# Six load buffers instead of four, and the first six pairs asked for at once, in cosine attention followed by a two-layer leaky-ReLU product

## The chip, the cores and the metric

The kernel runs on one core of a Trainium2 chip. The metric is the device time of one execution in microseconds. TensorE multiplies matrices and writes to PSUM (eight banks); VectorE (DVE), ScalarE (ACT) and GpSimd (POOL) do the elementwise work; SyncE (SP) only issues transfers. Sixteen DMA engines carry all transfers; they are asked for from SP, ACT or POOL, each with a queue of its own.

## The reference

```python
q_n = q / (norm(q, axis=-1) + 1e-6)          # q, k, v: 8 batches, 12 heads, 448 rows, 64 columns, f32
k_n = k / (norm(k, axis=-1) + 1e-6)
scores = q_n @ k_n.T / tau                   # tau = 0.1
attn = exp(scores - max) ; attn = attn / (sum(attn) + 1e-9)
x = (attn @ v) with the heads side by side   # 3584 tokens x 768
h = x @ w_in                                 # 768 x 2048
out = maximum(0.01 * h, h) @ w_out           # 2048 x 768, f32 out
```

Rows of q and k have length one, so the scores are bounded and the kernel leaves out the maximum.

## The kernel before, in words

**Tiling.** Two heads make a pair, called a slot: six slots to a batch, 48 in all. The 448 rows of a head are 3 x 128 (`MAIN`) and a remainder of 64. `load_qk(s)` (lines 119 to 132) asks for the q and k of a slot in four transfers: q main (192 KB, line 125), k main (192 KB, line 126), and the two remainders (32 KB each, line 128), which both go into the fourth column of the q tile. The tiles come from the pool `ld`, which has four buffers, so that slot s + 4 can be loaded when slot s is normalised. Two pairs of heads make a group of v, which `load_v(j)` brings in from POOL; `load_v_rem` brings in the remainders of v for a batch, `load_w_in(i)` one of four chunks of w_in, `load_w_out(half)` one of two halves of w_out, all from POOL, which casts them to bf16 on the way.

**The way of one slot.** `squares(s)` on POOL (line 165), `sums(s)` on VectorE (line 176), `roots(s)` on ScalarE (lines 183 to 186), `normalise(s)` on VectorE (lines 195 to 200), which writes `qn`; `transposes(s)` by TensorE for the first ten slots (line 214, copied out in line 238), by a DMA from SP after that (line 232). Then `key_tiles` (line 257) makes the scores of 128 keys at a time, ScalarE takes their exponential (line 269), `totals` and `products` (line 297, and 284 for remainders) make the sums and attn @ v, `scale` (line 332) divides. `hold(x)` (line 487) is a one-column copy on POOL; it makes POOL wait for x, and with it all that stands behind it in POOL's order, transfers too.

**The order.** It is written out by hand (`manual_schedule`): every engine executes its instructions in the order of the program. After the first loads and 22 warming matmuls on TensorE, slots 0 and 1 are prepared with help from ScalarE and VectorE. Then a loop over the six slots of batch 0 (line 528) has, in each step s: scores of slot s, normalisation of slot s + 1, the load of slot s + 5, the squares of slot s + 3 behind a hold, a load of v, w_in or w_out, and the transposes of slot s + 1. Then the stage of each batch b alternates two things. `firsts` (line 636) is the first product, x @ w_in (line 355), 16 blocks of d_ff, with preparations of later slots put between. `visit` (line 646) is the second product, g @ w_out (line 434), three or four groups of two row and column blocks, with the score tiles of the next batch put between; then `attend_batch` does the rest of that batch's attention. In the visit of batch 0 the order of the groups is chosen so that the first needs only the left half of w_out; the second also needs the right half. `norm(s)` (line 623) prepares a slot inside these stages: roots, normalisation, transposes, the load four slots on, and the squares two slots on.

**Around batch 0.** `norm(6)` and `norm(7)` load slots 10 and 11. `norm(8)` and `norm(9)`, placed between the blocks of the first `firsts` (lines 685 and 687), load nothing. In the first visit, `norm(10)` loads nothing, after the 16th block of the first group slots 12, 13 and 14 are loaded in a row (lines 663 to 665), and `norm(11)` loads slot 15; squares of slots 12 and 13 come with these (lines 661 to 667).

Of the kernel before, what the change touches and what calls it, by code (L numbers as in the profile page):

```python
# [9 lines left out]
BF16 = mybir.dt.bfloat16  # L10
# [6 lines left out]
def kernel(  # L17
# [10 lines left out]
    nc = tc.nc  # L28
# [15 lines left out]
    WARM = 22  # L44
    SOON = 4
    AHEAD = 3
    assert REM == 64 and D == 64 and H == 12

    ctx.enter_context(tc.manual_schedule())
    cpool = ctx.enter_context(tc.tile_pool(name="consts", bufs=1))  # L50
    ldp = ctx.enter_context(tc.tile_pool(name="ld", bufs=4))
    vbp = ctx.enter_context(tc.tile_pool(name="vb", bufs=4))
    sqp = ctx.enter_context(tc.tile_pool(name="sq", bufs=3))
    smp = ctx.enter_context(tc.tile_pool(name="small", bufs=3))
# [12 lines left out]
    gp = nc.gpsimd  # L67
# [36 lines left out]
    def load_w_in(i):  # L104
        n0, e = i // 2 * (D_ff // 2), i % 2
        gp.dma_start(
            out=w_in_sb[:, e::2, n0 : n0 + D_ff // 2], in_=w_in_r[e, :, :, n0 : n0 + D_ff // 2]
        )
# [5 lines left out]
    def main(x, b, h0, nh):  # L114
        return x[b, h0 : h0 + nh, 0:MAIN].rearrange("h (p t) d -> p h t d", t=3)

    raw = {}

    def load_qk(s, engs=(nc.sync, nc.sync)):
        if s >= NSLOT:  # L120
            return
        b, h0 = s // NPAIR, 2 * (s % NPAIR)
        q_h = ldp.tile([128, 2, 4, D], F32, name="q_h")
        k_h = ldp.tile([128, 2, 3, D], F32, name="k_h")
        engs[0].dma_start(out=q_h[:, :, 0:3], in_=main(q, b, h0, 2))
        engs[1].dma_start(out=k_h, in_=main(k, b, h0, 2))
        for i, (x, eng) in enumerate(zip((q, k), engs)):
            eng.dma_start(  # L128
                out=q_h[64 * i : 64 * i + 64, :, 3],
                in_=x[b, h0 : h0 + 2, MAIN:S].rearrange("h p d -> p h d"),  # L130
            )
        raw[s] = (q_h, k_h)
# [5 lines left out]
    def load_v(j):  # L138
        if j >= B * NQ:
            return  # L140
        b, jj = divmod(j, NQ)
        vb[j] = vbp.tile([128, 4, 3, D], BF16, name="v_b")
        gp.dma_start(out=vb[j], in_=main(v, b, 4 * jj, 4))  # L143
# [12 lines left out]
    def squares(s, engs=(gp, gp)):  # L156
        if s >= NSLOT:
            return
        tiles = []
        for x, eng, name in zip(raw[s], engs, ("sq0", "sq1")):  # L160
            sq = sqp.tile(list(x.shape), F32, name=name)
            if eng is nc.scalar:
                nc.scalar.activation(sq, x, func=AF.Square)
            else:
                eng.tensor_tensor(sq, x, x, op=ALU.mult)  # L165
            tiles.append(sq)
        sqs[s] = tiles
# [44 lines left out]
    def one(tp, s, lo, hi):  # L212
        for t in range(lo, hi):
            nc.tensor.matmul(  # L214
                out=tp[:, t, :],
                lhsT=qn[s][:, t].rearrange("p h d -> p (h d)"),
                rhs=id128,
                is_transpose=True,
                start=(t == lo),
                stop=(t == hi - 1),  # L220
            )

    def transposed():
        return banks(1).bitcast(BF16)[:, : 7 * 128].rearrange("p (t c) -> p t c", c=128)

    def transposes(s):
        if s >= NSLOT:
            return
        dst = qtp.tile([128, 7, 128], BF16, name="qkT")
        qkT[s] = dst.rearrange("p t c -> p (t c)")  # L230
        if s >= DMA_FROM:
            nc.sync.dma_start(
                out=dst, in_=qn[s].rearrange("p t h d -> p (t h d)"), transpose=True
            )
            return
        tp = transposed()
        one(tp, s, 0, 7)
        nc.vector.tensor_copy(out=dst, in_=tp)
# [210 lines left out]
                store(osb[c, ts], c, chunk_cols(c)[0] + ts * 128, 0, D_model)  # L449
        given_back(("rows", c, two))  # L450

    load_qk(0, (nc.sync, nc.scalar))
    load_qk(1, (nc.sync, gp))
    load_qk(2, (nc.sync, gp))
    load_qk(3)
    tiny = cpool.tile([128, 1], F32, name="tiny")
    nc.vector.memset(tiny, 1e-18)
    eps = cpool.tile([128, 1], F32, name="eps")
# [9 lines left out]
    for i in range(2):  # L468
        vrb.append(cpool.tile([128, NQ, 4, D], BF16, name=f"v_rem{i}"))
        nc.vector.memset(vrb[i], 0.0)  # L470
    id128 = cpool.tile([128, 128], BF16, name="id128")
    make_identity(nc, id128)


    def fill(count):
# [9 lines left out]
    def hold(x):  # L485
        seen = smp.tile([128, 1], F32, name="seen")
        gp.tensor_copy(out=seen, in_=x)  # L487

    hold(raw[1][1][:, 0, 0, 0:1])
    load_v_rem(0, slice(0, 2))  # L490
    load_w_in(0)


    (q_h, k_h), (q_h1, k_h1) = raw[0], raw[1]
# [14 lines left out]
    sums(1, (1,))  # L509
    nc.scalar.activation(sqs[1][0], q_h1, func=AF.Square)  # L510
    normalise(0)
    load_qk(4)
    hold(qn[0][:, 6, 0, 0:1])
    squares(2)
    load_v(0)
    dst = qtp.tile([128, 7, 128], BF16, name="qkT")
    qkT[0] = dst.rearrange("p t c -> p (t c)")
    for lo, hi, copy in ((0, 4, nc.scalar.copy), (4, 7, nc.vector.tensor_copy)):
# [9 lines left out]
    for s in range(NPAIR):  # L528
        j = s // 2 - 1 if s >= 2 else None
        even = s % 2 == 0  # L530
        n = s + 2 if s + 2 < NPAIR else None
        if s != 3 and s != 5:
            scores(s, (0,))
        if s == 1:
            roots(2)
        if j is not None and not even:
            products(j, 1)
        scores(s, (1,))
        fill(2)
        if s and n:  # L540
            sums(n, (0,))
        if s < 5:
            normalise(s + 1)
            load_qk(s + 5)
        if j is not None and not even:
            scale(j, 0)
        if s < 5:
            hold(qn[s + 1][:, 6, 0, 0:1])
            squares(s + 3)
        if s in (1, 2):  # L550
            load_v(s)
        if s == 0:
            load_v_rem(0, slice(2, 4))
        elif s in (1, 2, 3):
            load_w_in(s)
        if s in (3, 4):
            load_w_out(s - 3)
        if n:
            sums(n, (1,))
        scores(s, (2,))  # L560
        if s == 5:

            scale(j, 1)
            for m in range(SOON):
                pms[0, m] = banks(1, (0, m, 0), 4 + m)
            first(0, 0, range(KT - 2))
        elif not even:
            fill(2)
        if not even:
            scores(s, (3,))  # L570
        if s < 5:
            transposes(s + 1)
        if s == 0:
            sums(2, (0,))
        if s == 5:
            first(0, 1, range(KT - 2))
            sums(6)
            sums(7)
        elif not even:
            fill(2)  # L580
        if n and s:
            roots(n)
        if j is not None and not even and s < 5:
            scale(j, 1)
        if j is not None and even:
            totals(j)
            scores(s + 1, (0,))
            products(j, 0)
# [31 lines left out]
        attend(b * NQ + 2)  # L620


    def norm(s, transposed=True, load=True, ahead=2):
        if s >= NSLOT:
            return
        roots(s)
        normalise(s)
        if transposed:
            transposes(s)
        if load:  # L630
            load_qk(s + 4)
        hold(qn[s][:, 6, 0, 0:1])
        if ahead:
            squares(s + ahead)

    def firsts(b, begun, between):

        for m in range(begun, AHEAD):
            pms[b, m] = banks(1, (b, m, 0))
            first(b, m, range(KT - 2))  # L640
        for m in range(MT):
            for fn in between.get(m, ()):
                fn()
            first(b, m, range(KT - 2 if m < max(begun, AHEAD) else 0, KT))

    def visit(b, order, norms, between):


        s0 = (b + 1) * NPAIR
        tiles = [(s0 + p, ki) for p in range(NPAIR) for ki in range(3)]  # L650
        key_tiles([(s0 + 1, 3), (s0 + 3, 3)])
        for i, two in enumerate(order):
            after = between[i == len(order) - 1]
            for n, _ in enumerate(two_groups(b, two), 1):
                for _ in range(after.get(n, 0)):
                    key_tiles([tiles.pop(0)])
                if not tiles and s0 + 5 not in ended:
                    ended.add(s0 + 5)
                    key_tiles([(s0 + 5, 3)])
                if b == 0:  # L660
                    if n == 4 and i < norms:
                        norm(s0 + 4 + i, load=i, ahead=i)
                    if n == 16 and i == 0:
                        for s in range(3):
                            load_qk(s0 + 6 + s)
                    if n == 4 and i == norms:
                        squares(s0 + 7)
                elif n == 4 and i < norms:
                    norm(s0 + 4 + i)
                if n == 20 and i < norms:  # L670
                    sums(s0 + 5 + i)
        assert not tiles
# [9 lines left out]
    firsts(  # L682
        0, SOON, {
            5: [lambda: sums(8), lambda: transposes(6)],
            7: [lambda: norm(8, False, False), lambda: transposes(7)],
            8: [lambda: sums(9)],
            10: [lambda: norm(9, False, False), lambda: load_v(3)],
            11: [lambda: transposes(8), lambda: load_v(4)],
            13: [lambda: load_v(5), lambda: load_v_rem(1)],
            14: [lambda: transposes(9), lambda: sums(10)],  # L690
# [3 lines left out]
    for b in range(B):  # L694
# [15 lines left out]
        s = ready  # L710
# [50 lines left out]
```

## Time and profile before

| | us |
|---|---|
| median of 3 runs (418.15 to 420.12) | 418.28 |
| the profiled execution's own time | 417.95 |
| its span, from first to last instruction | 416.2 |
| TensorE busy | 402.5 (97%) |
| ScalarE busy | 259.9 (62%) |
| VectorE busy | 191.4 (46%) |
| POOL busy | 141.0 (34%) |
| moved by DMA, mean rate | 54.21 MB, 130 GB/s |

The page cuts the span into 40 slices of 10.4 us and gives a digit of the busy share for each; the last row of digits is that of the DMA engines. A bracket at the end of a timeline line gives the time that the engine sat idle before the instruction, and what ended it. "q1" is the queue of SP's transfers, "q10" that of ScalarE's, "q0" that of POOL's. A queue's row in the DMA view has packets, MB, and the time that its packets took as a share of 16 engines' time; shares of two queues overlap and can add to more than 100%. "To landing" is the time from a transfer's issue to its arrival.

### The profile page before, as it was taken

To read this page: it belongs to the slowest core of one execution; us is meant where nothing else is said; L and a number is where in the kernel's file an instruction comes from. 1 tells how busy PE (TensorE), PEld (TensorE's weight loads), DVE (VectorE), ACT (ScalarE), POOL (GpSimd) and SP (SyncE) were. 2 spreads that over 40 slices of the span, in tenths; PEclk is the share of its full clock that TensorE was granted. 3 is DMA by queue.
4 is the path that set the end of the run, shared out by engine and by line. 5 is a ranking of instruction groups with operands and counts; after the bars stand their busy time and mean duration, and the time that the engine had idled before them with its cause. 6 is when DMAs were issued, how large, how long until landed. Compare 5 with 4: busy or idle time off the path is not lost.

```text
span 416.2 us, 10171 instructions
## 1 busy us (share of the span) xinstructions
PE 402.5 (97%) x4099; PEld 215.0 (52%) x4099; DVE 191.4 (46%) x412; ACT 259.9 (62%) x448; POOL 141.0 (34%) x213
## 2 busy tenths in 40 slices
PE   7599999899999999999999999999999999999996
PEld 3234656444555555544555555544555565544564
DVE  6685862356362735157261645156362654040021
ACT  4687578645785569855775559855776559934300
POOL 6593563355240534054231533153232530000000
PEclk9999999999999999999999999999999999999999
DMA  8999999886475966576376875776477753210023
GB/s 195 185 173 219 220 210 209 217 116 131 95 199 126 115 157 123 121 121 141 90 179 143 115 172 93 138 110 136 108 173 161 104 95 55 70 39 2 0 76 77
DMA packets 104271, 54.21 MB, mean 130 GB/s; under 512 B 70560, under 2 KB 99104, under 8 KB 104224
## 3 DMA queue, kind: packets, MB, share of 16 engines
q1 hardware_dynamic: 78400, 40.98, 42.5%
q0 software_dynamic: 25248, 12.26, 23.1%
q8 instruction: 32, 0.52, 0.5%
q10 hardware_dynamic: 576, 0.33, 0.3%
q14 instruction: 15, 0.12, 0.1%
HBM read 45.61 MB, written 11.01 MB: 136 GB/s over the span
## 4 chain that ended last, share of the span: by engine, by line
PE 87%; DMA 5%; ACT 3%; DVE 2%; SPq 1%; POOL 1%; issue 1%; POOLq 0%
PE ps L355 34%; PE ps L434 27%; PE ps L297 12%; PE ps L257 7%; PE ps L392 5%; DMA q_h<-in_k_dram 3%; ACT pe L269 1%; DMA q_h<-in_q_dram 1%; PE ps L284 1%; DVE qn L200 1%; PE ps L214 1%; SPq L128 1%; POOL sq L165 1%; ACT pr L269 1%; PE ps L478 1%
## 5 line engine op out<-in xcount | busy, mean ns | idle before, releaser
L355 PE MATMUL ps<-xT,w_in_sb 128*128 128x384 bf16 (+1 forms) x768 | 147.7, 353 | 0.0
L434 PE MATMUL ps<-w_out_sb,hT 64*128 64x384 bf16 x1536 | 143.6, 323 | 0.4 <-DMA w_out_sb<-in_moe_w_out_dram 0.4
L269 ACT ACTIVATE pe<-ps 128x896 bf16<-128x896 f32 x144 | 123.4, 918 | 23.4 <-PE ps L257 21.7
L362 ACT ACTIVATE hT<-ps 128x384 bf16<-128x384 f32 (+1 forms) x128 | 67.7, 544 | 74.1 <-PE ps L355 73.9
L355 PEld LDWEIGHTS <-w_in_sb 128*128 128x128 bf16 x768 | 74.2, 98 | 71.2 <-issue 3.4
L434 PEld LDWEIGHTS <-hT 64*128 64x128 bf16 x1536 | 75.1, 94 | 54.8 <-issue 4.4
L176 DVE TENSOR_REDUCE ss<-sq 128x6 f32<-128x384 f32 (+1 forms) x95 | 54.6, 611 | 11.6 <-POOL sq L165 11.2
L257 PE MATMUL ps<-qkT 64*128 64x448 bf16 (+1 forms) x384 | 55.7, 356 | 4.0 <-DVE osb L444 1.7
L444 DVE COPY osb<-ps 128x384 f32<-128x384 f32 x48 | 24.5, 553 | 73.0 <-PE ps L434 39.8
L165 POOL TENSOR_TENSOR sq<-q_h 128x512 f32<-128x512 f32 x46 | 48.4, 1052 | 18.3 <-DMA q_h<-in_k_dram 17.7
L487 POOL CAST seen<-qn 128x1 f32<-128x1 bf16 x48 | 9.4, 196 | 130.5 <-DVE qn L200 124.1
L143 POOL DMA_DIRECT2D v_b<-in_v_dram x24 | 18.7, 778 | 62.0 <-PE ps L297 62.0
L195 DVE TENSOR_SCALAR ss<-ss 128x14 f32<-128x14 f32 x46 | 8.1, 175 | 67.9 <-ACT ss L184 67.9
L165 POOL TENSOR_TENSOR sq<-k_h 128x384 f32<-128x384 f32 x46 | 38.5, 838 | 0.0
L332 DVE TENSOR_TENSOR xT<-ps,rb 128x448 bf16<-128x448 f32 x48 | 27.8, 620 | 23.4 <-ACT rb L311 23.3
L200 DVE TENSOR_TENSOR qn<-q_h,r 128x512 bf16<-128x512 f32 x48 | 33.3, 694 | 1.6
L297 PE MATMUL ps<-pe,v_b 128*32 128x448 bf16 x576 | 32.0, 353 | 0.0
L257 PEld LDWEIGHTS <-qkT 64*128 64x128 bf16 (+1 forms) x384 | 17.6, 96 | 24.6 <-issue 11.6
L200 DVE TENSOR_TENSOR qn<-k_h,r 128x384 bf16<-128x384 f32 x48 | 28.2, 587 | 0.0
L310 ACT ACTIVATE rb<-ps 128x448 f32<-128x448 f32 x24 | 12.9, 539 | 23.1 <-PE ps L297 23.0
L297 PEld LDWEIGHTS <-v_b 128*32 128x32 bf16 x576 | 15.4, 97 | 11.8 <-issue 0.4
L398 DVE COPY osb<-ps 128x384 f32<-128x384 f32 (+1 forms) x9 | 4.6, 514 | 36.6 <-issue 22.6
(51 smaller groups left out, 225.7 us busy)
## 6 DMA issues: line engine op xcount, KB each, us to landing
q_h<-in_q_dram SPq DMA_DIRECT2D x48, 192.0 KB, 3.2
k_h<-in_k_dram SPq DMA_DIRECT2D x45, 192.0 KB, 3.5
out_dram<-osb SPq DMA_DIRECT2D x30, 192.0 KB, 3.0
v_b<-in_v_dram POOLq DMA_DIRECT2D x24, 192.0 KB, 4.6
out_dram<-osb SPq DMA_DIRECT2D x12, 384.0 KB, 2.9
w_in_sb<-in_moe_w_in_dram POOLq DMA_DIRECT2D x4, 768.0 KB, 11.5
w_out_sb<-in_moe_w_out_dram POOLq DMA_DIRECT2D x2, 1536.0 KB, 27.4
q_h<-in_q_dram SPq DMA_DIRECT2D x48, 32.0 KB, 3.8
```

The costliest lines, as they stand in the source:

```text
L165: eng.tensor_tensor(sq, x, x, op=ALU.mult)
L176: nc.vector.tensor_reduce(o.rearrange("p (h t) -> p h t", h=2), sqs[s][i], axis=AX.X, op=ALU.add)
L200: nc.vector.tensor_tensor(qn[s][:, lo:hi], x.rearrange("p h t d -> p t h d"), r[:, r0 : r0 + 2 * nt].rearrange("p (h t) -> p t h", h=2) .u ...
L257: nc.tensor.matmul(out=out[:, a, :S], lhsT=x[rows, c0:c1], rhs=x[rows, 0:S], start=True, stop=True,)
L269: nc.scalar.activation(out=dst, in_=sc[:, :, :S], func=AF.Exp, scale=inv_tau)
L297: nc.tensor.matmul(out=x[32 * g : 32 * g + 32, :S], lhsT=weights(g, ki) if ki < 3 else rem(g), rhs=pe[s][:, ki, a, :] if ki < 3 else pr[j] ...
L332: nc.vector.tensor_tensor(xT[m][:, 2 * jj + e, half * S : (half + 1) * S], pos.pop((j, e))[:, :S], rbs[j], op=ALU.mult,)
L355: nc.tensor.matmul(out=pm[:, :n], lhsT=w_in_sb[:, kt, m * 128 : (m + 1) * 128], rhs=xT[c // 2][:, kt, c0 : c0 + n], start=(kt == 0), stop= ...
L362: nc.scalar.activation(out=hT[c][:, m, :n], in_=pms.pop((c, m))[:, :n], func=AF.Prelu, alpha=0.01)
L392: nc.tensor.matmul(out=po2[:, :n], lhsT=hT[c][:, m, ts * 128 : (ts + 1) * 128], rhs=w_out_sb[:, m, lo : lo + n], start=(m == 0), stop=(m = ...
L434: last[i] = nc.tensor.matmul(out=po2[:, i, :HALF], lhsT=hT[c][rows, m, ts * 128 : (ts + 1) * 128], rhs=w_out_sb[rows, m, half * HALF : (ha ...
L444: nc.vector.tensor_copy(out=osb[c, ts][:, half * HALF : (half + 1) * HALF], in_=po2[:, i, :HALF])
```

## The change

The pool `ld` gets six buffers (`LOADS`), and every later load is asked for six slots ahead instead of four.

- At the start, slots 0 to 5 are asked for before anything else instead of slots 0 to 3. Slots 0 and 1 come from SP (q) and ScalarE (k); then POOL makes the identity matrix, which stood behind the constants before; slots 2 to 5 come from SP (q) and POOL (k). Before, only slot 0 used ScalarE, slots 1 and 2 used SP and POOL, slot 3 SP alone.
- The hold on slot 1's k on POOL, ahead of the first v remainders and of w_in's first chunk, is gone.
- The first chunk of w_in is asked for after the first squares and the first load of v; the other three one loop step earlier each.
- The loop loads slot s + 7 in step s instead of slot s + 5.
- Every `norm` loads slot s + 6 and squares slot s + 2; the special order in the visit of batch 0 is gone. So `norm(8)` to `norm(11)` now load slots 14 to 17, and `norm(6)` and `norm(7)` slots 12 and 13.

```diff
+    LOADS = 6
-    ldp = ctx.enter_context(tc.tile_pool(name="ld", bufs=4))
+    ldp = ctx.enter_context(tc.tile_pool(name="ld", bufs=LOADS))
...
-    load_qk(0, (nc.sync, nc.scalar))
-    load_qk(1, (nc.sync, gp))
-    load_qk(2, (nc.sync, gp))
-    load_qk(3)
+    for s in range(2):
+        load_qk(s, (nc.sync, nc.scalar))
+    id128 = cpool.tile([128, 128], BF16, name="id128")
+    make_identity(nc, id128)
+    for s in range(2, LOADS):
+        load_qk(s, (nc.sync, gp))
...
-    id128 = cpool.tile([128, 128], BF16, name="id128")
-    make_identity(nc, id128)
...
-    hold(raw[1][1][:, 0, 0, 0:1])
     load_v_rem(0, slice(0, 2))
-    load_w_in(0)
...
-    load_qk(4)
+    load_qk(LOADS)
     hold(qn[0][:, 6, 0, 0:1])
     squares(2)
     load_v(0)
+    load_w_in(0)
...
-            load_qk(s + 5)
+            load_qk(s + 1 + LOADS)
...
-        elif s in (1, 2, 3):
-            load_w_in(s)
+        if s < 3:
+            load_w_in(s + 1)
...
-    def norm(s, transposed=True, load=True, ahead=2):
+    def norm(s, transposed=True):
...
-        if load:
-            load_qk(s + 4)
+        load_qk(s + LOADS)
         hold(qn[s][:, 6, 0, 0:1])
-        if ahead:
-            squares(s + ahead)
+        squares(s + 2)
...
-                if b == 0:
-                    if n == 4 and i < norms:
-                        norm(s0 + 4 + i, load=i, ahead=i)
-                    if n == 16 and i == 0:
-                        for s in range(3):
-                            load_qk(s0 + 6 + s)
-                    if n == 4 and i == norms:
-                        squares(s0 + 7)
-                elif n == 4 and i < norms:
+                if n == 4 and i < norms:
                     norm(s0 + 4 + i)
...
-            7: [lambda: norm(8, False, False), lambda: transposes(7)],
+            7: [lambda: norm(8, False), lambda: transposes(7)],
...
-            10: [lambda: norm(9, False, False), lambda: load_v(3)],
+            10: [lambda: norm(9, False), lambda: load_v(3)],
```

## The prediction

> **What bounds the kernel now.** I read the page first, then the waits of the first 81 us, the chain in order of time, the timeline at the places the chain named, and last the DMA view by stretches. The page:
>
> ```profile
> PE 402.5 (97%) x4099; PEld 215.0 (52%) x4099; DVE 191.4 (46%) x412; ACT 259.9 (62%) x448; POOL 141.0 (34%) x213
> ...
> PE   7599999899999999999999999999999999999996
> ...
> DMA  8999999886475966576376875776477753210023
> ```
>
> TensorE is busy in 402.5 of 416.2 us. Only slices 1, 2 and 8 (0 to 21 and 73 to 83 us) leave it idle, and DMA is near full up to about 70 us. So the change can act in the first 80 us only; later loads wait for nobody. The waits of the first 81 us, then the two longest pieces of the chain, then the instructions there:
>
> ```profile
> POOL sq L165 <- DMA q_h<-in_k_dram: 17.7, 6, 5.0
> ...
> PE ps L434 <- DMA w_out_sb<-in_moe_w_out_dram: 0.4, 1, 0.4
> ```
>
> ```profile
> 7.96 8.00 DMA q_h<-in_k_dram
> ...
> 65.52 5.93 DMA q_h<-in_k_dram
> ```
>
> ```profile
> 16.13 1.03 POOL L165 TENSOR_TENSOR sq<-q_h 128x512 f32<-128x512 f32 x1 [3.68 <-DMA q_h<-in_k_dram]
> ...
> 19.04 0.97 PE L214 MATMUL ps<-id,qn 128*128 128x128 bf16 x7 [2.73 <-DVE qn L200]
> ...
> 29.70 1.19 POOL L112 DMA_DIRECT2D w_out_sb<-in_moe_w_out_dram  x1
> ...
> 35.57 1.21 POOL L112 DMA_DIRECT2D w_out_sb<-in_moe_w_out_dram  x1
> ...
> 64.13 0.97 PE L434 MATMUL ps<-w_out_sb,hT 64*128 64x384 bf16 x9 [0.38 <-DMA w_out_sb<-in_moe_w_out_dram]
> ...
> 74.45 0.81 PE L257 MATMUL ps<-qkT 64*128 64x448 bf16 x2 [1.66 <-DVE osb L444]
> ```
>
> The fourth pair (slot 3) lands at 15.96, because its last piece was issued at 7.96, behind SP's wait for an earlier load, and then shared the engines with the first w_in chunk; TensorE idles 2.73 us for it. Slot 12, asked for in the first visit, lands at 71.45; its squares hold up VectorE, whose copies then free a bank 1.66 us late. Both stalls are what early loads would remove. The line at 64.13 is the one to keep in mind: the second half of w_out, issued at 35.57, lands at 64.07 (28.5 us to landing, the longest in that tile's answer), and TensorE reaches it at just that time. The first half lands at 56.0 (29.70 + 26.3, the shortest), 1.1 us before its first use at 57.08.
>
> DMA by stretch: 15 to 25 us, then the queues of 45 to 55 us, then of 57.75 to 60.75 us, in which w_out runs alone (columns of a queue: packets, MB, share):
>
> ```profile
> DMA  9999999999843211079495899964410096589999
> ```
>
> ```profile
> q0 software_dynamic: 1698, 1.30, 82.5%
> q1 hardware_dynamic: 1595, 0.90, 41.8%
> ```
>
> ```profile
> q0 software_dynamic: 800, 0.61, 131.7%
> ```
>
> Idle tenths of the first line (9 taken as full) add up to 12.3 slices of 0.25 us: 3.1 us of free DMA. After 25 us the engines are never free before w_out is in. While SP's queue (q1, loads) and POOL's (q0, weights) both have work, they take packets nearly one to one.
>
> **The change part by part.**
>
> *The front.* POOL gets the identity first (0.25 + 0.29 us, from 4.11 to 1.3 us), then eight load DMAs for four, at 0.91, 0.63, 0.75 and 0.63, mean 0.73: 8 x 0.73 = 5.8. It ends at about 7.7, with the two v_rem DMAs (1.26) at 9.0, just before the 9.21 at which it takes up the first normalised pair: that wait hides it, with 0.2 us of cover; without it, each us late would delay slot 2's squares by one. ACT issues four DMAs instead of two (0.48 + 0.74 each), done by 3.3, before its first square at 4.01. SP issues twelve; in the trace it is held for an earlier load's landing at its ninth (7.31, just after the second pair's q at 7.30). From the third pair on it will be held in this way, to about 9.5; slot 6 queues behind, and nobody needs it before 25. The second pair's k, now on POOL's queue, goes behind the first pair's on ACT's; its square on ACT at 6.34 stands ahead of the roots of pair 0. It may land as late as pair 2's k, 2.79 + 4.4 (that row's median to landing) = 7.2: 0 to 1.0 us for everything, take 0.5.
>
> *The fourth pair.* It lands by about 11.5. Its squares then start after load_v(0), w_in(0)'s issue (0.8, moved there) and the hold at 12.27: at 13.3 instead of 16.13. Next late is the normalisation of slot 2, which needs its roots (end 15.07, with the front's 0.5 at 15.6) and began at 17.80: 2.2 us gained. The clock row shows more:
>
> ```profile
> 15.40:18.80 3.40, 0.58 (x5) 0.21 (x4) 1.53 (x4) 2.10 (x3) 2.67 (x4) 1.00 0.92 201
> 18.80:22.20 3.40, 3.16 (x15) 1.06 (x15) 3.01 (x8) 1.32 (x3) 2.97 (x5) 0.50 0.72 151
> ...
> 64.13:79.64 15.51, 13.73 (x157) 8.59 (x156) 4.18 (x10) 11.55 (x15) 4.91 (x8) 1.00 1.19 209
> ...
> 161.70:175.20 13.50, 13.50 (x182) 7.42 (x180) 4.89 (x12) 11.71 (x16) 2.78 (x4) 1.00 0.68 167
> ```
>
> (Stretch, length, busy PE, PEld, DVE, ACT, POOL, granted clock, DMA share, GB/s.) After 3.4 us with TensorE 17% busy, the granted clock was 0.50 for 3.4 us; seven transposes took 0.97 there and 0.77 at 11.82. Without the gap I count 0.5 back. Of 40 to 57.08, TensorE is busy 16.64 of 17.08; squares that waited for loads there wait no more: 0 to 0.4, take 0. So TensorE reaches w_out 2.2 + 0.5 = 2.7 us earlier, the second half at 61.4.
>
> *Weights.* w_in(0) goes from 7.04 to about 12.5, w_in(1) to (3) one step earlier; the engines stay full from then, so the 3.1 us of idle are won. v_rem and v of batch 0 now queue behind one more w_in chunk: 0 to 1.5 us of TensorE around 25 and 36, which only shortens the wait below.
>
> *Loads ahead of w_out.* Slots 4 and 5 only change places within the first 25 us. But slots 12 to 15, asked for from 62.67 on, are now asked for by the normalisations of 6 to 9 (42.1, 44.6, about 48 and 53, less 2.7), while w_out is on its way. Price: alone, w_out gets 800 packets in 3 us, 267 per us; the 1698 of 45 to 55 us would take 6.4, leaving 3.6 us for 1595 load packets, 443 per us. A pair has 768 data packets (192 KB twice in rows of 768 bytes, 32 KB twice in rows of 256) and its completions, some 830: 1.9 us. The bounds are 1.2 (448 KB at the 369 GB/s of the slice at 3 us, with loads alone) and 1.9; I take 1.8, nearest to the row with w_out beside it. Slots 10 and 11 took 5 us each beside w_out (their squares start on landing, at 52.84 and 57.76); at that pace 12 to 14 land by 62 and 15 around 67. So three to four pairs come in between: 64.1 - 3.1 + 5.4 to 7.2 = 66.4 to 68.2. I take 67.0, the lower side, since part of slot 15 falls behind. TensorE waits 5.6 us there, in order, with the score tiles behind it, and so ACT.
>
> By the Trainium skill, DMA: Bandwidth & Descriptors, section on queues, rings and completion order, each engine goes round robin between queues at packet granularity; 1698 against 1595 agrees, and w_out cannot keep the loads out.
>
> *After the wait.* The second and third group of the first visit took 79.64 - 64.51 = 15.1 us, the undisturbed ones 13.5: 1.6 gained. A wait of 5.6 us holds a stretch as idle as 15.4 to 18.8, so the clock should halve once for 3.4 us: 0 to 1.7, take 1.0. The Trainium skill, TensorE: Matmul & The Clock Gate, Part 1, asks for one idle window of about 3.4 us, free-running; by that an idle 5.6 us holds a whole one in two of three cases, which as an estimate gives 1.1; the row's drop came with 17% activity.
>
> **Sum.** The second group starts at 67.0 instead of 64.5: +2.5; - 1.6; + 1.0: +1.9. The profiled execution took 417.95 us (span 416.2 and 1.75 around it), 0.33 under the median of 418.28. So 419.9 for it, 420.2 for a median.
>
> **Rivals.** *A, w_out in time:* the loads fit the freed time, because SP, held at its in-flight limit, asks for 14 and 15 too late to be in the way, or a pair costs 1.2 us. Then 2.7 + 1.8 (15.51 - 13.73) = 4.5 gained: 413.8. For: 3.1 us of idle and a rise from 205 to 222 GB/s when loads join w_out. Against: full engines from 25 to 64 and landings within 1.1 us of need. It decides where w_out's second half lands before 63.5. Between, at 65, is +0.5 - 1.6: 417.2.
> *B, the front loses:* pair 0 or 1 lands 1 to 2 us late with six pairs asked for at once. ACT's square at 6.34 and the roots behind it carry the delay to everything up to w_out, whose chunks are issued later too: 421 to 422.5. For: DMA is already full then, 0.87 MB in 3 to 6 us at a mean of 292 GB/s. Against: each queue serves pairs 0 and 1 first. The Trainium skill's rules for kernel authors on the same DMA page say spreading over issuing engines saves only issue time.
> *C, it doesn't do what it says:* slot 3 is still late because SP is held; 2.7 falls to nothing, w_out is late all the same: about 420, as the wait swallows it.
>
> **How the numbers follow.** Forecast case 0.62 (0.02 faster, 0.27 same, 0.33 slower), own range 417.5 to 422.5; A 0.20 (0.17 faster, 0.03 same); B 0.10 (slower); C 0.08 (0.05 same, 0.03 slower). A measurement tells about 0.5% from no change, 2.1 us here. Sums: faster 0.19, same 0.35, slower 0.46. The range goes down into A, to 414.5, and up to 423.0 with B.
>
> **What would show it.** POOL's squares of slot 3 start near 13.3 with no wait; no clock of 0.50 at 19 to 22; no stall at 74. Against that, an L434 matmul waits 4 to 6 us for w_out_sb near 61, and w_out's second DMA lands at 66 to 68. Landing before 63.5 makes A right and me wrong; a square of slot 1's k after 7.3 speaks for B.

## The result, and the profile after

The changed kernel takes 421.59 us (median of 20 runs, 418.4 to 423.27), the kernel before 418.82 (20 runs, 415.31 to 420.35). The ratio is 1.0063, with a 95% interval of 1.0043 to 1.0083: slower by 0.6%. The profiled execution took 423.18, at the upper end of the kernel's runs, with a span of 421.4. So its differences from the trace before add up to 5.2 us of span, about twice the difference of the medians; how much of that is chance stays open, as told below.

The page of the changed kernel (line numbers are one higher than before in most of the code):

```profile
PE 403.7 (96%) x4088; PEld 215.5 (51%) x4099; DVE 190.5 (45%) x412; ACT 260.2 (62%) x448; POOL 142.3 (34%) x216
...
PE   6789994999999999999999999999999999999996
...
DMA  8999999976568674866567675766566632310023
```

The seventh digit of TensorE, 63 to 74 us, is a 4; behind it TensorE's row is the same as before. The waits of the first 85 us:

```profile
PE ps L435 <- DMA w_out_sb<-in_moe_w_out_dram: 5.5, 1, 5.5
...
POOL v_b L144 <- DMA w_out_sb<-in_moe_w_out_dram: 1.4, 1, 1.4
```

POOL's waits for loads (17.7 us before) are gone from the head of this list, and the wait for w_out has grown from 0.4 to 5.5. The same places in the timeline, front first:

```profile
5.47 0.62 ACTq L129 DMA_DIRECT2D q_h<-in_k_dram  x1
6.14 0.52 ACT L497 ACTIVATE sq<-q_h 128x384 f32<-128x384 f32 x1 [4.12 <-DMA q_h<-in_q_dram]
...
9.04 0.52 ACT L506 ACTIVATE sq<-k_h 128x384 f32<-128x384 f32 x1 [1.87 <-DMA k_h<-in_k_dram]
9.47 0.29 ACT L184 ACTIVATE ss<-ss,tiny 128x14 f32<-128x14 f32 x1
...
15.51 1.05 POOL L166 TENSOR_TENSOR sq<-q_h 128x512 f32<-128x512 f32 x1
...
57.59 0.98 PE L435 MATMUL ps<-w_out_sb,hT 64*128 64x384 bf16 x10
...
69.75 1.75 PE L435 MATMUL ps<-w_out_sb,hT 64*128 64x384 bf16 x9 [5.50 <-DMA w_out_sb<-in_moe_w_out_dram]
```

Two things happened. At the front, ScalarE's fourth transfer was issued only at 5.47, and its first square, which had started at 4.01, came right behind it at 6.14; the square of the second pair's k started at 9.04 instead of 6.34; the roots of slot 0, behind it in ScalarE's order, started at 9.47 instead of 6.79. The squares of slot 3 (15.51) wait for no load any more. TensorE reaches w_out at 57.6 instead of 57.1. Then the second half of w_out holds it from 64.25 to 69.75. The stretches of that wait and of the two groups behind it (columns as in the prediction: length, busy PE, PEld, DVE, ACT, POOL, granted clock, DMA share, GB/s; the granted clock is the share of TensorE's full speed, so that 0.50 is half speed):

```profile
64.25:69.75 5.50, 0.00 (x1) 0.00 (x0) 3.44 (x8) 0.73 (x3) 2.01 (x3) 0.77 1.41 175
69.75:85.14 15.39, 15.39 (x163) 9.31 (x167) 1.02 (x2) 11.12 (x13) 0.82 (x1) 0.86 1.03 149
```

The two groups take 15.4 us with TensorE busy throughout, where undisturbed ones take 13.5. The rest is mainly the clock, 0.86 over the stretch. It was halved from 67.2 to 74.0, from inside the wait on, and TensorE worked 4.25 us at half speed:

```profile
63.80:67.20 3.40, 0.45 (x5) 0.07 (x2) 3.00 (x7) 1.18 (x3) 0.34 (x2) 1.00 1.28 219
67.20:70.60 3.40, 0.85 (x6) 0.48 (x7) 0.56 (x2) 0.00 (x0) 2.02 (x3) 0.50 1.52 138
67.20:74.00 6.80, 4.25 (x28) 2.39 (x29) 0.56 (x2) 0.92 (x1) 2.49 (x3) 0.50 1.44 174
...
69.75:73.20 3.45, 3.45 (x22) 1.95 (x23) 0.00 (x0) 0.92 (x1) 0.82 (x1) 0.50 1.37 198
```

### The profile page after: what moved, and what is told of

Its sections match the earlier page's. It is cut to its first block, busy times and chain, and to the rows that moved or that the text cites. A ratio compares the mean times of both kernels' runs of the same rounds, so it can differ in the third digit from the quotient of the medians.

```text
span 421.4 us, 10157 instructions
## 1 busy us (share of the span) xinstructions
PE 403.7 (96%) x4088; PEld 215.5 (51%) x4099; DVE 190.5 (45%) x412; ACT 260.2 (62%) x448; POOL 142.3 (34%) x216
## 4 chain that ended last, share of the span: by engine, by line
PE 84%; DMA 11%; POOL 2%; DVE 2%; issue 1%; ACT 0%; SPq 0%; POOLq 0%
PE ps L356 31%; PE ps L435 29%; PE ps L298 10%; DMA w_out_sb<-in_moe_w_out_dram 8%; PE ps L258 7%; PE ps L393 5%; DMA q_h<-in_k_dram 1%; PE ps L285 1%; POOL sq L166 1%; DVE qn L201 1%; DMA q_h<-in_q_dram 1%; PE ps L215 0%; POOL v_rem L151 0%; PE ps L479 0%; DVE r L197 0%
## 5 line engine op out<-in xcount | busy, mean ns | idle before, releaser
L435 PE MATMUL ps<-w_out_sb,hT 64*128 64x384 bf16 x1536 | 145.6, 326 | 5.5 <-DMA w_out_sb<-in_moe_w_out_dram 5.5
L435 PEld LDWEIGHTS <-hT 64*128 64x128 bf16 x1536 | 75.8, 95 | 60.9 <-issue 8.8
L258 PE MATMUL ps<-qkT 64*128 64x448 bf16 (+1 forms) x384 | 56.6, 359 | 2.5 <-ACT pe L270 1.2
L201 DVE TENSOR_TENSOR qn<-k_h,r 128x384 bf16<-128x384 f32 x48 | 27.3, 569 | 0.0
L270 ACT ACTIVATE pr<-ps 128x896 bf16<-128x896 f32 x24 | 21.3, 923 | 0.2 <-PE ps L258 0.2
```

The costliest lines, as they stand in the source:

```text
L201: nc.vector.tensor_tensor(qn[s][:, lo:hi], x.rearrange("p h t d -> p t h d"), r[:, r0 : r0 + 2 * nt].rearrange("p (h t) -> p t h", h=2) .u ...
L258: nc.tensor.matmul(out=out[:, a, :S], lhsT=x[rows, c0:c1], rhs=x[rows, 0:S], start=True, stop=True,)
L270: nc.scalar.activation(out=dst, in_=sc[:, :, :S], func=AF.Exp, scale=inv_tau)
L435: last[i] = nc.tensor.matmul(out=po2[:, i, :HALF], lhsT=hT[c][rows, m, ts * 128 : (ts + 1) * 128], rhs=w_out_sb[rows, m, half * HALF : (ha ...
```

## The experiments

All times to landing of w_out's second half below are its issue in the timeline plus the longest time to landing that the profile gives for that tile. "Attention starts" is the first remainder matmul of batch 1 (line 284 or 285), at which the early part of the kernel is over; all kernels run alike behind it. Ratios are against the kernel before, run beside them; its median was 418.82 beside the changed kernel, 418.51 beside e1 to e4 and 418.12 beside e5 to e8, so ratios compare better across these groups than medians. The second column leaves out a pair that was asked for in the last microseconds before w_out landed: slot 12 in the kernel before (from 62.67 on), slot 14 in e8 (from 63.23), slot 16 in the changed kernel, e2 and e4 (from 65.09, 62.94 and 64.83).

| kernel | pairs 12 to 15 asked for ahead of w_out's end | w_out lands | attention starts | span | median | ratio (95%) |
|---|---|---|---|---|---|---|
| before | none | 64.1 | 79.6 | 416.2 | 418.82 | 1 |
| changed | 4 | 69.7 | 85.1 | 421.4 | 421.59 | 1.0063 (1.0043 to 1.0083) |
| e1: pairs late, five in a row | none | 60.1 | 85.5 | 421.8 | 423.41 | 1.0108 (1.0081 to 1.0135) |
| e2: slot 1's k from POOL | 4 | 66.2 | 82.0 | 418.4 | 420.12 | 1.0032 (1.0013 to 1.0050) |
| e3: e1 and e2 | none | 59.1 | 85.6 | 422.0 | 422.95 | 1.0099 (1.0068 to 1.0130) |
| e4: matmuls in the wait | 4 | 67.8 | 81.8 | 418.1 | 419.93 | 1.0033 (1.0013 to 1.0052) |
| e5: pairs late, spread | none | 60.9 | 76.5 | 412.8 | 414.50 | 0.9911 (0.9891 to 0.9932) |
| e6: e5, lighter front | none | 59.7 | 74.9 | 411.1 | 412.95 | 0.9881 (0.9858 to 0.9904) |
| e7: 12, 13 early | 2 | 64.4 | 77.7 | 414.0 | 415.44 | 0.9938 (0.9916 to 0.9959) |
| e8: before, 12, 13 early | 2 | 67.5 | 82.4 | 419.0 | 421.93 | 1.0085 (1.0053 to 1.0116) |

The theory after the result was that of the prediction: the pairs asked for six ahead take turns on the DMA engines from w_out, TensorE waits for w_out, and the clock halves after the wait. The rival was the front, which had come out 2.7 us late where 0.5 had been allowed.

**e1: the pairs asked for late.** Slots 12 to 16 in the first visit, as the kernel before does with its own:

```diff
+    def norm(s, transposed=True, load=True, ahead=2):
...
-    norm(6, False)
+    norm(6, False, False)          # the same for 7, 8 and 9: no load
...
+                if b == 0:
+                    if n == 4 and i < norms:
+                        norm(s0 + 4 + i, load=i, ahead=i)
+                    if n == 16 and i == 0:
+                        for s in range(0, 5):
+                            load_qk(s0 + 6 + s)
+                    if n == 4 and i == norms:
+                        squares(s0 + 7)
```

> The changed kernel, with slots 12 to 16 asked for inside the first visit, after the sixteenth block of its first group, and not by norm(6) to norm(10). Theory (loads ahead of w_out set the end): four pairs fewer in front of w_out's second half, 4 x 1.8 = 7.2 us, so it lands near 62.5 instead of 69.7 and the second group, due at 64.3, waits under 1 us; the half clock after it is gone too (1.9), while the stall of the kernel before near 74 comes back (1.7). 5.5 + 1.9 - 1.7 = 5.7 less in the profiled execution; median 416 to 418. Rival (the late front alone sets the loss): w_out still lands near 69 and the median stays at 420.5 to 422.

Measured: 423.41 us, slower than the changed kernel. Half of the expectation held: w_out landed at 60.1, and the second group, due near 62.4 (55.70 + 6.7), started without a wait. The other half fell to a wait that neither theory had:

```profile
75.34 1.28 SPq L233 DMA_TRANSPOSE qkT<-qn  x1
...
78.95 0.93 PE L258 MATMUL ps<-qkT 64*128 64x448 bf16 x4 [7.15 <-DMA qkT<-qn]
```

(Timeline of e1.) Slot 11's transposes are a transfer on SP, and stood behind five pairs, twenty transfers, which kept SP from 61.35 to 75.23; their issues in the timeline add up to 12.0 us. The scores of slot 11 waited 7.15 us for them, with the clock halved behind. So removing the wait for w_out did not show in the time, because the experiment made a new one of its size. e1 alone proves neither theory.

**e2: the front.** Slot 1's k from POOL:

```diff
-    for s in range(2):
-        load_qk(s, (nc.sync, nc.scalar))
+    load_qk(0, (nc.sync, nc.scalar))
+    load_qk(1, (nc.sync, gp))
```

> The changed kernel, with slot 1's k asked for from POOL again, so that ScalarE issues two transfers instead of four. Both theories: ScalarE's first square starts near 4.0 instead of 6.14, and the first normalised pair is there 1.5 to 2.7 us earlier. Theory (w_out): it lands within 1 us of 69.7, TensorE waits the longer for it, median 420.5 to 422.5. Rival (front): the 2 us go through to the end, median 418.5 to 420.

Measured: 420.12 us. ScalarE's first square started at 3.97, POOL's hold for slot 0 passed at 9.81 instead of 11.88, and TensorE was at w_out at 54.8 instead of 57.6. The time lies a little under the theory's 420.5 to 422.5 and over the rival's 418.5 to 420; the theory's landing was wrong: w_out came at 66.2, not within 1 us of 69.7. POOL asks for w_in and w_out in its order behind the first squares, so an earlier front also starts the bulk earlier (first w_in chunk at 12.54 instead of 14.61). But the wait stayed: 

```profile
66.26 1.76 PE L435 MATMUL ps<-w_out_sb,hT 64*128 64x384 bf16 x9 [4.74 <-DMA w_out_sb<-in_moe_w_out_dram]
```

(Timeline of e2.) So the late front is not the cause of the wait. It may be a part of the loss: the medians differ by some 1.5 us, but the intervals overlap, and e1, whose front is that of the changed kernel, reached w_out at 55.7 in its profile, so most of the difference between the two arrivals can be chance.

**e3: both edits together.**

> The changed kernel with both edits: slots 12 to 16 asked for in the first visit, slot 1's k from POOL. Theory: w_out's second half lands near 62, due near 62, so that the front's 2 us now count: 1 to 2 us under the run with late loads alone, median 414.5 to 416.5, under the kernel before. Rival (front alone): as the run with slot 1's k from POOL, 418.5 to 420.

Measured: 422.95 us, as e1 and for its reason: w_out lands at 59.1, and slot 11's transposes, issued at 76.10 behind the five pairs, hold TensorE for 7.26 us. TensorE reached w_out at 55.9, not earlier than in e1 (55.7). Inconclusive on the front.

**e4: the clock.** 20 matmuls of the warming tile ahead of the second group, so that TensorE is not idle in its wait:

```diff
             after = between[i == len(order) - 1]
+            if b == 0 and i == 1:
+                fill(20)
```

> The changed kernel, with 20 matmuls of the warming tile put ahead of the second group of the first visit, so that TensorE works for some 4 us while it waits for w_out. Theory (the idle wait halves the clock): w_out lands at 69.7 as before, the granted clock stays at 1.00 after it, the two groups behind it take 13.5 instead of 15.4 us: median 419.5 to 420.2. Rival (the clock costs nothing, the score exponentials on ScalarE set the pace): 421 to 422.5.

Measured: 419.93 us, inside the theory's range. The filling matmuls ran from 63.18 to 67.67, no wait for w_out is left to see, and the clock held behind them:

```profile
67.60:81.90 14.30, 13.69 (x165) 8.50 (x169) 1.02 (x2) 11.12 (x13) 1.24 (x2) 1.00 1.15 173
```

(A stretch of e4.) The two groups took 14.3 us, not 13.5: a wait of 0.61 for slot 11's transposes is in it. w_out landed at 67.8 here, 1.9 earlier than in the changed kernel's profile, with no edit ahead of it; ScalarE's first square started at 5.24 instead of 6.14 and the first w_in chunk was issued 0.5 us earlier. So a part of the 1.7 us between the medians can be of that kind. What e4 shows is that the clock stays whole behind the wait when TensorE is kept at work; what this is worth in the median it does not show.

**e5: late and spread.** e1's wait taken away: slot 12 behind the first group, 13 and 14 behind slot 11's transposes, 15 to 17 in the last group (the diff is against e1):

```diff
-                        norm(s0 + 4 + i, load=i, ahead=i)
-                    if n == 16 and i == 0:
-                        for s in range(0, 5):
-                            load_qk(s0 + 6 + s)
+                        norm(s0 + 4 + i, load=False, ahead=i)
+                    for s in {(0, 16): (12,), (1, 4): (13, 14), (2, 16): (15, 16, 17)}.get((i, n), ()):
+                        load_qk(s)
```

> The changed kernel, with slot 12 asked for after the sixteenth block of the first visit's first group, 13 and 14 behind slot 11's transposes in the second, 15 to 17 in the third. Theory (w_out behind the pairs, and SP's order behind that): w_out's second half lands near 60, no wait at the second group (start near 63), slot 11's transposes no longer behind five loads, so no stall at its scores: the batch's attention starts near 76.6 instead of 85.1 in the changed kernel and 79.6 in the kernel before. Median 414.5 to 416.5. Rival (asking for 12 to 17 late costs as much wherever it is put): 418.5 or more.

Measured: 414.5 us, 0.9911 of the kernel before, as the theory said. TensorE has no gap from 57 to 80 us and the clock is whole:

```profile
57.00:80.00 23.00, 23.00 (x320) 12.93 (x320) 9.10 (x20) 20.37 (x30) 7.98 (x13) 1.00 1.04 186
```

(A stretch of e5.) This is the changed kernel with one thing undone, the place of six pairs (the squares of slots 12 and 13 move behind them). 421.59 - 414.5 = 7.1 us of the medians hang on it, 6.4 by the ratios; 5.5 of wait and 1.9 of clock in the changed kernel's profile are 7.4.

**e6: a lighter front on top of it.** Slot 0's k from ScalarE, 1 to 3 from POOL, 4 and 5 from SP alone (the diff is against e5):

```diff
-    for s in range(2):
-        load_qk(s, (nc.sync, nc.scalar))
+    load_qk(0, (nc.sync, nc.scalar))
+    load_qk(1, (nc.sync, gp))
...
-        load_qk(s, (nc.sync, gp))
+        load_qk(s, (nc.sync, gp if s < 4 else nc.sync))
```

> As the run with the late pairs spread, and with a front of fewer transfers on POOL and ScalarE: slot 0's k from ScalarE, 1 to 3 from POOL, 4 and 5 from SP alone. Theory: ScalarE's first square near 4.0, POOL free some 1.5 us earlier, TensorE at w_out 1.5 to 2.5 us earlier (near 54), w_out landing near 59: median 413 to 415.5, 1 to 2 below the spread run. Rival (POOL's or SP's queue gives it back): within 0.7 of the spread run.

Measured: 412.95 us, just under the theory's range, 1.55 below e5 and 1.2% below the kernel before: the fastest of all. ScalarE's first square starts at 4.14, POOL's hold for slot 0 passes at 8.86, TensorE is at w_out at 55.1, and w_out lands at 59.7 with the second group due near 61.8. With w_out in time, the front's gain goes through to the end. Which of the two edits to the front brought it was not tried.

**e7: two pairs early.** As e5, but norm(6) and norm(7) load slots 12 and 13:

> The changed kernel, with slots 12 and 13 asked for by norm(6) and norm(7) as in it, and 14 to 17 late. Price of a pair: with four pairs early w_out's second half landed at 67.8 and 69.7, with none at 60.1; if a pair costs 1.9 to 2.4 us each, two give 64 to 65, a wait of 1 to 2 us, little loss of clock. Median 416 to 418. Rival (only the last pair before w_out matters, or all four are one effect of order): landing within 1 us of 60 or of 68.

Measured: 415.44 us, below the 416 to 418 expected, with the landing (64.4) and the wait (1.29) as expected:

```profile
64.46 0.97 PE L435 MATMUL ps<-w_out_sb,hT 64*128 64x384 bf16 x9 [1.29 <-DMA w_out_sb<-in_moe_w_out_dram]
```

(Timeline of e7.) With none early w_out landed at 60.1 and 60.9 (e1, e5), with two at 64.4: a pair puts it off by 1.7 to 2.1 us. With four it was 67.8 and 69.7, 1.7 (67.8 - 60.9) to 2.4 us (69.7 - 60.1) a pair, but there slot 16 came in for a part too. e2 and e3, which share a front, give 1.8 (66.2 - 59.1, over four), slot 16 included.

**e8: the kernel before, two pairs early.** Only the change's loading ahead, with four buffers and the old front:

```diff
-            7: [lambda: norm(8, False, False), lambda: transposes(7)],
+            7: [lambda: norm(8, False), lambda: transposes(7)],
...
-            10: [lambda: norm(9, False, False), lambda: load_v(3)],
+            10: [lambda: norm(9, False), lambda: load_v(3)],
...
-                        for s in range(3):
-                            load_qk(s0 + 6 + s)
+                        load_qk(s0 + 8)
```

> The kernel before, four buffers, its own front, with one edit: norm(8) and norm(9) load slots 12 and 13 (14 and 15 as before, in the first visit). Theory: w_out's second half lands at 64.1 + 2 x 1.9 to 2.4 = 67.9 to 68.9, TensorE waits 3.5 to 4.5 us for it, the clock halves once (1 to 1.9), slot 12's stall near 74 goes (1.7): +3 to +4, median 421.3 to 422.8, without any of the change's front. Rival (it takes six buffers or the new front to lose): 417 to 419.

Measured: 421.93 us, in the theory's range, and as slow as the whole change. w_out landed at 67.5, a little before the 67.9 to 68.9 expected, and TensorE waited:

```profile
67.49 0.97 PE L434 MATMUL ps<-w_out_sb,hT 64*128 64x384 bf16 x9 [3.82 <-DMA w_out_sb<-in_moe_w_out_dram]
```

(Timeline of e8.) 67.5 - 64.1 = 3.4 us for two pairs, 1.7 each. The clock was halved behind the wait, for 3.4 us:

```profile
65.30:68.70 3.40, 1.21 (x16) 0.86 (x17) 1.95 (x4) 0.02 (x1) 2.44 (x4) 1.00 1.43 161
68.70:72.10 3.40, 3.40 (x24) 1.95 (x22) 0.11 (x1) 1.82 (x2) 2.08 (x3) 0.50 1.35 222
```

(Stretches of e8.) Neither six buffers nor the new front is needed for the loss.

## Why the prediction was right, and where its terms were off

The forecast of 420.2 (+1.9 us) stands against 421.59 (+2.8): slower, by the cause named, somewhat more than forecast. The terms came out worse than the total: the profiled execution, in which they are read, lost 5.2 us and not 1.9, because the gains counted ahead of w_out did not arrive. That the median came nearer is in part luck.

*Loads ahead of w_out:* right. The price of a pair was put at 1.8 us; e8 measured 1.7 in the old kernel, e7 1.7 to 2.1 in the new. w_out was not asked for late: its second half was issued at 34.38, before at 35.57. By the queue rows of 45 to 55 us, 1667 packets against 1667 in the changed kernel, the two queues moved equal numbers; this agrees with the round robin that the Trainium skill gives (DMA: Bandwidth & Descriptors, queues, rings and completion order). The 3.1 us of idle DMA were won too: with no pair early, w_out landed at 60.1 and 60.9 instead of 64.1. The sum of 66.4 to 68.2 was missed in the profiled execution (69.7) and met in e4 (67.8), which has the same order up to there. The sum left out slot 16, which `norm(10)` asks for from 65.09 on, and it had no late front. But e4 has slot 16 too, and its first w_in chunk came only 0.5 us earlier, so most of the 1.9 us between the two landings is not explained.

*The wait:* 5.6 us forecast, 5.5 measured, but both of its ends stood 2.7 to 2.9 us later than forecast, 64.25 and 69.7 for 61.4 and 67.0. The agreement is partly luck: both ends were late by about as much. The prediction also misread one line: it put the start of the second group before at 64.51, which is 64.13 with the wait of 0.38 added, but that wait lies ahead of the start. So the group was due at 63.75, with 2.7 us gained at 61.05, and by the prediction's own terms the wait is nearly 6 us. In the sum the slip cancels: 67.0 is 2.9 behind 64.13, and the two groups, which took 15.5, get 2.0 shorter, which with 1.0 for the clock is +1.9 again.

*The front:* the term that failed. "0 to 1.0 us for everything, take 0.5" was 2.7 at the first normalised pair (POOL's hold for slot 0 passed at 11.88 instead of 9.21). The prediction had seen that SP's ninth transfer waits for an earlier landing, and had ScalarE done with its four transfers by 3.3. ScalarE's fourth was issued at 5.47, just when SP's second, issued at 1.26, had landed:

```profile
1.26 4.19 DMA q_h<-in_q_dram
...
5.47 5.17 DMA q_h<-in_k_dram
```

(Chain of the changed kernel.) ScalarE's first square stood behind it, at 6.14. The square of slot 1's k started at 9.04, and the k was forecast by 7.2.

*Rival B* had named this place, at 1 to 2 us. Its sign, that square after 7.3, came true, and 421.59 lies in its range of 421 to 422.5 as well. What decides is e5: its front is late too (that square at 8.80), and it is 0.9% faster than the kernel before. And e8 has the old front and is as slow as the change.

*The fourth pair:* the mechanism held (squares at 15.51 with no wait, no stall in front of the transposes of slot 2, TensorE at full clock from 18.8 to 22.2). Its 2.7 us did not reach w_out: the front took them, and TensorE arrived 0.5 later than before instead of 2.7 earlier. The clock's drop did not go away either in this profile, it moved forward, to 12.6 to 16.0, behind the new idle time of the front:

```profile
9.20:12.60 3.40, 1.13 (x10) 0.61 (x10) 2.74 (x6) 2.45 (x7) 0.72 (x2) 1.00 1.12 248
12.60:16.00 3.40, 3.40 (x17) 1.04 (x15) 1.99 (x5) 3.05 (x6) 3.40 (x6) 0.50 0.69 164
```

(Stretches of the changed kernel.) In the profile of e7, whose order is the same up to there, the clock stayed whole. e6 suggests, by one profile, what the fourth pair is worth with a front that keeps it: TensorE at w_out at 55.1, 2.0 before the old 57.1.

*After the wait:* 13.5 us was about right for the two groups, and the clock added 1.9 to them where 1.0 was taken and 1.7 was the bound. What was wrong is "halve once for 3.4 us": the clock was halved from 67.2 to 74.0, twice as long; in the first half of that time TensorE worked only 0.85 us. 4.25 us of work at half speed cost 2.1 us, and 15.4 less 2.1 is 13.3. The Trainium skill's rule of one idle window (TensorE: Matmul & The Clock Gate, Part 1) would have it in two of three cases for a wait of 5.6 us; it came in the changed kernel, in e2 and in e8, and not in e7, which waited only 1.29 us. In e8 the 3.4 us ahead of it held 1.21 us of work, so here the stretch was not wholly idle. e4, which kept TensorE busy, had no halving there.

*Rival A* (w_out in time) fell: its deciding landing of 63.5 was met by no kernel that asked for two or four of the pairs early. *Rival C* had the total about right for the wrong place: slot 3 was in time.

What stays open is how much the front varies by itself: ScalarE's first square stood at 6.14, 5.90, 5.24, 5.40 and 6.19 in the profiles of five kernels whose order is the same up to there (the changed one, e1, e4, e5, e7), and one profile of each cannot say how often. It may be a reason that the profiled execution lost 5.2 us and the median 2.8, but this was not tested, and e7, with the latest of these squares, reached w_out 1.1 us before the changed kernel. Open, too, is what the clock costs over many runs. The mean granted clock of each of the changed kernel's 20 runs is on record, 0.980 to 0.996; 3.4 us at half speed take 0.004 off such a mean, so that is five stretches to one. The five runs at 0.996, with only one, took 420.74 to 422.28 us, no less than the others.

## What to carry to other kernels

Loading further ahead is not free while DMA is full: ask which transfer lands just in time now (here the second half of w_out, due at 63.75, which is 64.13 less its wait of 0.38, and landed at 64.07), and count each transfer that is put beside it at its price. Pairs that nobody needs yet belong behind it, and not all in a row, so that a short transfer on the same queue, like slot 11's transposes, doesn't stand behind them. And an engine that computes should issue few transfers at a time when many are in flight, since a transfer that has to wait for an earlier landing holds the computation behind it, as ScalarE's fourth did here.

## What the runs showed of the hardware that was not expected

- ScalarE's fourth transfer was issued at 5.47, 2.6 us behind its third (2.08 + 0.84), and its square followed at 6.14, 2.1 later than with two transfers (3.97 in e2, 4.01 before).
- Twenty transfers in a row on SP took from 61.35 to 75.23 in e1, 0.7 us each, most of it issue time; the transposes behind them landed just before 78.95.
- The clock halved behind stretches of 3.4 us in which TensorE was busy for 0.45 us (63.8 to 67.2) and 1.13 us (9.2 to 12.6) in the changed kernel, 1.21 us (65.3 to 68.7) in e8 and 0.58 us (15.4 to 18.8) before; in none of these cases was the stretch wholly idle. It stayed halved for 3.4 us, or, behind longer waits, for two or three times that (6.8 in the changed kernel, 10.2 in e1).
